# Routing records ten rows apart, tiles of successive ranks, and weighted rows written as one piece, in a fused attention and mixture-of-experts kernel

## The chip, the cores and the metric

The kernel runs on one core of a Trainium2 chip. The metric is device time in microseconds (us), the median over runs. TensorE is PE, VectorE is DVE, ScalarE is ACT, GpSimd is POOL and SyncE is SP in the profile; PEld is TensorE's weight load.

## The reference

Two parts follow each other. Attention with pooled keys and values (8 batches, 8 heads, 576 positions of 64 numbers; keys and values are means over 8 positions) gives x, 4608 tokens of 512 numbers. Then a noisy gate picks two of eight experts per token, and each expert is a two-layer network:

```python
attn = softmax(scale * q @ k_p.T)             # k_p, v_p: mean over 8 positions
x = (attn @ v_p) as (4608, 512)
noisy = x @ w_gate + log1p(exp(x @ w_noise)) * noise
top2, top2_w = two largest of noisy, softmax of the two
for e in range(8):
    for k in range(2):
        mask = top2[:, k] == e
        h = maximum(x[mask] @ w1[e], 0)       # w1: 512 x 1024
        out[mask] += top2_w[mask, k, None] * (h @ w2[e])   # w2: 1024 x 512
```

## The kernel before, in words

**Attention.** The batches are taken as four pairs. Each pair is nine chunks of 128 rows of q. The background work of a later batch (pooling of k and v, L230; block tiles `vbd`, L307 and L322) goes in between the chunks. For a chunk, PE makes scores `s`, DVE their maximum `mx` (L375), ACT the exponentials `ex` (L377), PE their transposes `ep` (L388) and the product `a` (L403), and DVE scales it to `xr` (L409, L410, L414), which is written to `x_dram`. L416 writes the chunk's gate logits into `lg`.

**Routing.** After a pair's last chunk, `route` (L480 on) turns `lg` into records. POOL adds the heads' logits (L490, L491), DVE starts with L494, and after the top-two choice `mb` (L544) PE counts ranks (`rk`, L571). DVE then works out, for each token and each of its two experts, the rank of the token among those of the expert, and the position of its record, `pos` (L594). A record is four words: the token, its weight, the row of the output if this is the token's second expert, and the slot in which the row of its first expert lies (the mate). The record's last word is written by L612. Then 18 indirect DMAs of POOL (`scatter`, L615: one chunk, one choice, 128 records of 16 bytes) write the records to `rec_dram`. They stand in a list, `scq`, and are issued one or two at a time during the next pair's chunks. Thirteen of a pair's scatters stand on POOL ahead of L490 and L491 of the next pair's route, five behind them. Each engine takes its instructions in order.

**Records in memory.** Expert e has ER = 4672 rows of `rec_dram`, and rank r lies in row e*ER + r. `load_recs` (L643 on) brings them to `raw` by sections of 4, 3, 2 and 1 tiles (4, 2, 3 and 1 for expert 0): in a section of n tiles that starts at tile ts, partition p of tile t gets rank ts*128 + p*n + (t - ts). The two first loads of expert 0 go on POOL after the second and the third pair; the rest, six DMAs, on SP after the fourth (L656). Tile 9 has 64 rows only; two memsets (L652) clear the rest.

**Experts.** From about 222 us PE multiplies. A group is 2 to 4 tiles of an expert. The rows of x are gathered by the records (`xg` by L683 for expert 0, `row` by L692 for the others). `stage1` (L964) makes `ph`, ACT `hh` and DVE `hl` of it (L971, L972), and `stage2` (L1071, or L1037 for an expert's last group) makes `py` or `xp`. Each product is three matmuls of reduced precision. `prev` (L992) gathers the mate's rows from `slot_dram` into `pv`, and `finish` (L1008) weights the tile and adds them, writes the result to `slot_dram` (L1012, on POOL) and scatters it to `out` (L1016, on POOL). The slot of rank r is 128 + e*1216 + r, so L1012 writes 128 rows that lie n rows apart. An expert's last group is computed for one of three numbers of columns, by how many records there are (`by_rows`, `tail`).

```python
ts, n = [x[:2] for x in (SECT if e else SECT0) if x[0] <= t][-1]
turn_of("pool", lambda: nc.gpsimd.dma_start(bass.AP(
    tensor=slot_dram.tensor, offset=slot_dram.offset + (P + e * CAP + ts * P + t - ts) * DM,
    ap=[[n * DM, np_], [1, DM]]), res[:np_]))
```

Of the kernel before, what the change touches and what calls it, by code (L numbers as in the profile page):

```python
# [19 lines left out]
def kernel(  # L20
# [36 lines left out]
    OVR = ER - CAP  # L57
    VW = D + 2 * E + 1
    assert (H, D, G, E, S, DM, NTOK) == (8, 64, 72, 8, 576, 512, 4608)

# [14 lines left out]

    x_dram = dp.tile([NTOK, DM], F32, name="x_dram")
    rec_dram = dp.tile([E * ER, RW], I32, name="rec_dram")
    slot_dram = dp.tile([P + E * ER, DM], F32, name="slot_dram")

    ident = cp.tile([P, P], F32, name="ident")  # L80
    make_identity(nc, ident)
# [395 lines left out]
    def route(pr, c0, c1, lg, psum):  # L477
# [69 lines left out]
        def word(w):  # L547
            return rec[:, :n, :, w].rearrange("p n i -> p i n")
# [55 lines left out]
        V.scalar_tensor_tensor(slot, ei, -float(OVR), jump, op0=OP.mult, op1=OP.add)  # L604
        V.tensor_add(key, key, ei)
        later = t(2, NCH)
        for i in range(2):
            V.tensor_tensor(later[:, i], key[:, i], key[:, 1 - i], op=OP.is_gt)
            V.scalar_tensor_tensor(word(3)[:, i], slot[:, 1 - i], float(P - E * OVR), later[:, i],
                                   op0=OP.add, op1=OP.mult)  # L610
        V.tensor_scalar(later, later, -BIG, BIG + float(pr * 2 * S), op0=OP.mult, op1=OP.add)
        V.tensor_add(word(2), later, tb)  # L612
# [17 lines left out]
            for i in range(2):  # L630
                scq.append(lambda c=c, i=i: scatter(c, i))
        if pr == NP // 2 - 1:
            scq.append(lambda: load_recs(0, 1, 0, 1, 1))
            scq.append(lambda: fetch(groups[0]))
        if pr == NP - 2:
            scq.append(lambda: load_recs(0, 1, 1, 2, 2))
            scq.append(lambda: fetch(groups[1]))
        if pr == NP - 1:
            scq.append(lambda: load_recs(0, 1, 2, 4))
            scq.append(lambda: fetch(groups[2]))  # L640
            scq.append(lambda: load_recs(1, E, 0, 4))

    def load_recs(e0, e1, s0, s1, early=0):  # L643
        ne = e1 - e0
        sect = SECT if e0 else SECT0
        t0, t1 = sect[s0][0], sect[s1 - 1][0] + sect[s1 - 1][1]
        nt = t1 - t0
        nm = f"{e0}_{t0}"
        V = nc.vector
# [3 lines left out]
        src = rec_dram.rearrange("(e r) c -> e (r c)", e=E)  # L653
        for ts, n, np_ in sect[s0:s1]:
            o = ts * P * RW
            ld = (nc.gpsimd if RE >> (0 if early else 1 if e0 == 0 else 2) & 1 else nc.sync).dma_start(raw[:np_, :, ts - t0:ts - t0 + n].rearrange("p e t c -> p e (t c)"),  # L656
                                   src[e0:e1, o:o + np_ * n * RW].rearrange("e (p x) -> p e x", p=np_))
            if early:
                tc.add_to_no_dep_group(f"rec_load{early - 1}", ld.ins)
# [337 lines left out]
    def finish(e, t, np_, y, pv, plain=0):  # L997
        res = y if plain else pv
        wc = wcol[e, t][:plain or np_]
        if not plain:  # L1000
            rv = res[:np_].rearrange("p (u m c) -> p u m c", u=4, c=32)
            yv = y[:np_].rearrange("p (m u c) -> p u m c", u=4, c=32)
            parts = [(rv[:, u], yv[:, u]) for u in range(4)]
        else:
            parts = [(res[:plain], y[:plain])]
        for r_, y_ in parts:
            if e:
                nc.vector.scalar_tensor_tensor(r_, y_, wc, pv[:plain] if plain else r_, op0=OP.mult, op1=OP.add)  # L1008
            else:
                pace[0] = nc.vector.tensor_scalar(r_, y_, wc, None, op0=OP.mult)  # L1010
        ts, n = [x[:2] for x in (SECT if e else SECT0) if x[0] <= t][-1]
        turn_of("pool", lambda: nc.gpsimd.dma_start(bass.AP(  # L1012
            tensor=slot_dram.tensor, offset=slot_dram.offset + (P + e * CAP + ts * P + t - ts) * DM,
            ap=[[n * DM, np_], [1, DM]]), res[:np_]))
# [149 lines left out]
    nc.vector.tensor_scalar(sg[:, 0:1], red[:, 0:1], float(ER), float(CAP), op0=OP.mult, op1=OP.add)  # L1164
    nc.vector.scalar_tensor_tensor(sg[:, 0:1], sg[:, 1:2], float(P), sg[:, 0:1], op0=OP.mult, op1=OP.add)
    NTAB = 64
    nc.vector.scalar_tensor_tensor(sg[:, 1:2], red[:, 0:1], -float(CAP), sg[:, 0:1], op0=OP.mult, op1=OP.add)
    nc.vector.tensor_single_scalar(sg[:, 1:2], sg[:, 1:2], float(P + (E - 1) * CAP), op=OP.add)
# [21 lines left out]
    with tc.For_i(0, totr, 1) as it:  # L1190
# [1 line left out]
                             max_val=E * ER - P)  # L1192
        er = nc.values_load(tabr[0:1, bass.ds(it * 3 + 1, 1)], engines=[SPE], min_val=0, max_val=E - 1)
        slot = nc.values_load(tabr[0:1, bass.ds(it * 3 + 2, 1)], engines=[SPE], min_val=P + E * CAP,
                              max_val=E * ER)
# [64 lines left out]
```

## Time and profile before

| What | Value |
| --- | --- |
| runs | 1083.31, 1078.56, 1077.47 us; median 1078.56 |
| profiled execution, its own time | 1077.82 us |
| its span in the trace | 1076.0 us |
| mean granted clock of PE | 0.972 |
| busy share of PE, DVE, ACT, POOL | 94%, 51%, 32%, 35% |
| chain that ended last: PE, DMA, DVE, issue, ACT, POOL | 79%, 6%, 5%, 4%, 3%, 2% |

The busy shares say that PE is close to always at work. The chain that ended last follows the work back from the end: a share of it on an engine other than PE is time in which that engine, and not PE, set the end. A row of a timeline gives start, duration, engine, line, operation, output<-input, and in brackets how long the engine had been idle and what ended that.

### The profile page before, as it was taken

The numbers are of one execution on the slowest core, as the hardware profiler recorded it, in microseconds if no ns is written. First come the engines' busy times: TensorE is split into PE (matmuls) and PEld (weight loads), VectorE is DVE, ScalarE is ACT, GpSimd is POOL, SyncE is SP. The second block draws the span as 40 slices with busy tenths as digits, with TensorE's granted clock in tenths as the row PEclk, the third lists the DMA queues.
The fourth block names the chain that finished last, engine by engine and source line by source line (L and its number), as shares of the span: only waits on it lengthen the run. The fifth ranks groups of instructions, "written<-read, shape, count | busy, mean of one in ns | idle before, by whom it ended". The sixth has DMA issues, their size and how long they took to land.

```text
span 1076.0 us, 16501 instructions
## 1 busy us (share of the span) xinstructions
PE 1006.3 (94%) x5832; PEld 895.7 (83%) x5832; DVE 548.1 (51%) x1261; ACT 347.6 (32%) x857; POOL 375.7 (35%) x421
## 2 busy tenths in 40 slices
PE   7889788889899999999999999999999999999996
PEld 6778777668789898889898988898889888988895
DVE  5678675576134463563346435634463446455342
ACT  4677657533122231332133213221322132223120
POOL 3002735445610234154214530633063305431414
PEclk8999999889899999999999999999999999999998
DMA  9999842545351776476446754764377447754623
GB/s 268 234 265 250 223 130 61 146 112 166 83 150 44 198 235 185 134 231 209 135 116 215 237 149 130 246 218 140 111 250 229 146 116 238 241 164 144 199 95 131
DMA packets 136006, 187.61 MB, mean 174 GB/s; under 512 B 29123, under 2 KB 84052, under 8 KB 135898
## 3 DMA queue, kind: packets, MB, share of 16 engines
q1 hardware_dynamic: 110458, 119.09, 39.2%
q0 software_dynamic: 25440, 67.05, 20.2%
q8 instruction: 72, 1.18, 0.5%
q14 instruction: 36, 0.29, 0.1%
HBM read 123.31 MB, written 70.74 MB: 180 GB/s over the span
## 4 chain that ended last, share of the span: by engine, by line
PE 79%; DMA 6%; DVE 5%; issue 4%; ACT 3%; POOL 2%; SPq 0%; another core or an unknown queue 0%; POOLq 0%; ACTq 0%; DVEq 0%
PE ph L964 36%; PE py L1071 16%; PE xp L1071 9%; PE py L1037 6%; PE xp L1037 3%; PE a L403 2%; DMA wst<-in_moe_w_dram 2%; DMA qr<-in_q_dram 2%; PE qp L342 1%; PE s L370 1%; PE ep L388 1%; DMA v<-in_v_dram 1%; ACT ex L377 1%; DVE w L464 1%; DVE k L230 1%
## 5 line engine op out<-in xcount | busy, mean ns | idle before, releaser
L964 PE MATMUL ph<-xh,w 128*128 128x512 f32 (+6 forms) x1536 | 400.6, 342 | 19.9 <-DVE hl L972 14.8
L964 PEld LDWEIGHTS ph<-xh,w 128*128 128x128 f32 x1536 | 275.3, 191 | 46.6 <-issue 13.7
L964 PE MATMUL ph<-xl,w 128*128 128x512 f32 (+6 forms) x768 | 262.0, 341 | 0.2
L971 ACT ACTIVATE hh<-ph 128x512 fp32r<-128x512 f32 (+4 forms) x192 | 97.6, 509 | 495.8 <-PE ph L964 346.2
L972 DVE SCALAR_TENSOR_TENSOR hl<-ph,hh 128x512 fp32r<-128x512 f32 (+4 forms) x192 | 110.0, 579 | 226.5 <-ACT hh L971 197.5
L1071 PE MATMUL py<-w,hh 128*128 128x512 f32 x592 | 184.6, 390 | 0.0
L964 PEld LDWEIGHTS ph<-xl,w 128*128 128x128 f32 x768 | 146.3, 190 | 12.3 <-issue 1.1
L1071 PEld LDWEIGHTS py<-w,hh 128*128 128x128 f32 x592 | 110.6, 188 | 21.9
L1071 PE MATMUL py<-w,hl 128*128 128x512 f32 x296 | 115.4, 390 | 0.0
L615 POOL DMA_INDIRECT rec_dram<-rec,pos x72 | 79.1, 1098 | 66.5 <-issue 14.6
L1012 POOL DMA_DIRECT2D slot_dram<-pv x55 | 31.8, 579 | 184.7 <-DVE pv L1008 157.1
L1008 DVE SCALAR_TENSOR_TENSOR pv<-py,raw,pv 128x128 f32<-128x128 f32 x124 | 35.1, 342 | 110.9 <-PE py L1071 65.8
L1012 POOL DMA_DIRECT2D slot_dram<-yt x17 | 9.8, 577 | 229.5 <-DVE yt L1008 176.2
L1071 PE MATMUL xp<-w,hh 128*128 128x512 f32 x288 | 89.5, 390 | 0.0
L992 POOL DMA_INDIRECT pv<-slot_dram,raw x70 | 68.1, 972 | 59.6 <-DMA slot_dram<-ys 33.3
L464 DVE TENSOR_TENSOR w<-wst,w 128x512 fp32r<-128x512 f32 x128 | 84.2, 695 | 7.8 <-ACT w L463 6.5
L463 ACT CAST w<-wst 128x512 fp32r<-128x512 f32 x128 | 72.7, 617 | 21.5 <-DMA wst<-in_moe_w_dram 20.9
L692 POOL DMA_INDIRECT row<-x_dram,raw x70 | 70.6, 1008 | 21.6 <-issue 21.0
L403 PE MATMUL a<-vbd,eT 112*128 112x162 f32 (+3 forms) x480 | 70.8, 313 | 5.4 <-ACT eT L390 2.8
L377 ACT ACTIVATE ex<-s,mx 128x72 f32<-128x72 f32 x288 | 70.0, 338 | 17.9 <-DVE mx L375 14.4
L403 PEld LDWEIGHTS a<-vbd,eT 112*128 112x128 f32 (+1 forms) x480 | 64.1, 195 | 9.7 <-ACT eT L390 5.1
L898 ACT CAST xh<-xt 128x512 fp32r<-128x512 f32 (+1 forms) x70 | 42.0, 600 | 91.8 <-DVE xt L893 61.0
(168 smaller groups left out, 1324.5 us busy)
## 6 DMA issues: line engine op xcount, KB each, us to landing
wst<-in_moe_w_dram SPq DMA_DIRECT2D x64, 512.0 KB
via<-row SPq DMA_DIRECT2D x266, 64.0 KB
xg<-via SPq DMA_DIRECT2D x63, 256.0 KB
slot_dram<-pv POOLq DMA_DIRECT2D x55, 256.0 KB
x_dram<-xr SPq DMA_DIRECT2D x16, 512.0 KB
q<-in_q_dram SPq DMA_DIRECT2D x7, 1024.0 KB
k<-in_k_dram SPq DMA_DIRECT2D x6, 896.0 KB
v<-in_v_dram SPq DMA_DIRECT2D x12, 432.0 KB
```

What stands on the lines that cost most here:

```text
L377: lasta[0] = nc.scalar.activation(ex[:, jj, EPOS[h] * G:(EPOS[h] + 1) * G], sv[:, i], AF.Exp, bias=mx[:, i:i + 1])
L403: nc.tensor.matmul(a[ts_, half, (hs[0] % 4) * VW:(hs[-1] % 4 + 1) * VW], eT[:BST, n, ts_], vb[:BST, SLOT0[n]:SLOT0[n] + len(hs), :], start ...
L463: nc.scalar.copy(hv, sv)
L464: nc.vector.tensor_sub(lv, sv, hv.bitcast(F32))
L615: s = nc.gpsimd.indirect_dma_start(out=rec_dram[:, :], out_offset=bass.IndirectOffsetOnAxis(ap=pos[:, i, c:c + 1], axis=0), in_=rec[:, c, ...
L692: turn_of("pool", lambda: nc.gpsimd.indirect_dma_start(out=row[:32 * nr], out_offset=None, in_=x_dram[:, :], in_offset=bass.IndirectOffset ...
L964: nc.tensor.matmul(part(ph), w1s(e, a, db, f), part(xs[b][:, db]), start=(i == 0), stop=(i == 3 * NDB - 1))
L971: act = nc.scalar.activation(hh[:, :n], ph[:, :n], AF.Relu)
L972: last = nc.vector.scalar_tensor_tensor(hl[:, :n], ph[:, :n], 0.0, hh[:, :n].bitcast(F32), op0=OP.max, op1=OP.subtract)
L992: turn_of("pool", lambda: nc.gpsimd.indirect_dma_start(out=pv[:np_], out_offset=None, in_=slot_dram[:P + e * CAP, :], in_offset=bass.Indir ...
L1037: nc.tensor.matmul(part(py), w2s(e, b, f)[:, mb * P:(mb + 1) * P], part(hs[f][a]), start=(i == 0), stop=(i == 3 * NFB - 1))
L1071: mm = nc.tensor.matmul(py, hs[f][a][:, cs], w2s(e, b, f), start=(i == 0), stop=(i == 3 * NFB - 1))
```

## The change

Rank r below 1216 now has its record in row e*ER + (r mod 128)*10 + r div 128, so successive ranks lie ten records apart, and partition p of tile t gets rank t*128 + p. Ranks from 1216 on move up by 64 rows (GAP); ER becomes 4736. `pos` needs r mod 128 and so a cast, an AND and more arithmetic: ten DVE instructions (L595 to L608) stand where three stood (L594 to L597), each of 128x18. `raw` is loaded with one DMA per call, so SP has two instead of six, and the memsets are gone. L1012 becomes a write of consecutive rows. Slot numbers are the same. The narrowest form of `tail` takes one run of columns: 368 instead of 3 pieces of 124 for expert 0, and 240 instead of 2 of 120 for the others. Where the pad is written, 592 instead of 584 KB are. The cut diff:

```diff
-    ER = CAP + OV_T * P
+    NT = 10
+    GAP = NT * P - CAP
+    ER = CAP + GAP + OV_T * P
...
+        rr = t(2, NCH)
+        V.scalar_tensor_tensor(rr, ei, -float(ER), pf, op0=OP.mult, op1=OP.add)
+        V.tensor_scalar(key, rr, float(CAP + E * ER), float(E), op0=OP.is_ge, op1=OP.mult)
+        low = t(2, NCH, dt=I32)
+        V.tensor_copy(low, rr)
+        V.tensor_single_scalar(low, low, P - 1, op=OP.bitwise_and)
+        lin = t(2, NCH)
+        V.scalar_tensor_tensor(lin, low, float(NT * P - 1), rr, op0=OP.mult, op1=OP.add)
+        V.scalar_tensor_tensor(lin, ei, float(P * ER), lin, op0=OP.mult, op1=OP.add)
+        V.tensor_scalar(lin, lin, 1.0 / P, float(E * ER - E * ER // P), op0=OP.mult, op1=OP.add)
+        far = t(2, NCH)
+        V.scalar_tensor_tensor(far, pf, float(GAP), lin, op0=OP.add, op1=OP.subtract)
+        V.scalar_tensor_tensor(far, far, 1.0 / E, key, op0=OP.mult, op1=OP.mult)
-        V.tensor_copy(pos[:, :, :n], pf)
-        key = t(2, NCH)
-        V.scalar_tensor_tensor(key, ei, -float(ER), pf, op0=OP.mult, op1=OP.add)
-        V.tensor_scalar(key, key, float(CAP + E * ER), float(E), op0=OP.is_ge, op1=OP.mult)
+        V.tensor_add(pos[:, :, :n], lin, far)
...
-        if s1 == len(SECT):
-            V.memset(raw[64:, :, nt - 1, :], 0)
-        for ts, n, np_ in sect[s0:s1]:
-            ld = (...).dma_start(raw[:np_, :, ts - t0:ts - t0 + n]..., src[e0:e1, o:o + np_ * n * RW]...)
+        src = rec_dram.rearrange("(e r) c -> e (r c)", e=E)[e0:e1, :NT * P * RW]
+        ld = (nc.gpsimd if early else nc.sync).dma_start(
+            raw.rearrange("p e t c -> p e (t c)"),
+            src.rearrange("e (p x) -> p e x", p=P)[:, :, t0 * RW:t1 * RW])
...
-        if w == 80:
-            n = 120 if e else 124
-            return ap[:, :k * P].rearrange("p (t c) -> p t c", c=P)[:, :, :n]
         return ap[:, :k * P + 64 - w]
...
+        r0 = P + e * CAP + t * P
+        turn_of("pool", lambda: nc.gpsimd.dma_start(slot_dram[r0:r0 + np_], res[:np_]))
```

A scheduler decides where the routing's DVE instructions stand among those of the attention. POOL has the same instructions in the same order as before up to the expert stage. On DVE the order moves. First the end of the first pair's route, before (`rec` is the record, L612 its last word; the names that end in numbers are of single tiles):

```order
L609 SCALAR_TENSOR_TENSOR rec_0_1003<-rt_0_24_1155,rt_0_25_1158 128x9 x2
L416 TENSOR_TENSOR lg_848<-a_2_2_0_1225,rd_2_2_0_1238 128x128
L611 TENSOR_SCALAR rt_0_25_1158<-rt_0_25_1158 128x18
L375 TENSOR_REDUCE mx_3_1_0_1266<-s_3_1_0_1262 128x6
L612 TENSOR_TENSOR rec_0_1003<-rt_0_25_1158,tok_107 128x2x9
L375 TENSOR_REDUCE mx_3_1_1_1279<-s_3_1_1_1275 128x6
L307 TENSOR_TENSOR vbd_163<-vs_1121,vmask 112x8x64
L409 TENSOR_SCALAR rd_3_0_0_1295<-a_3_0_0_1288 128x8
L307 TENSOR_TENSOR vbd_163<-vs_1121,vmask 112x2x64
L410 RECIPROCAL rd_3_0_0_1295<-rd_3_0_0_1295 128x8
L230 TENSOR_TENSOR k_189<-k_189 128x5x128
```

The same place on DVE in the changed kernel, where `pos` is L608 and the record's last word L623:

```order
L375 TENSOR_REDUCE mx_3_1_1_1290<-s_3_1_1_1286 128x6
L608 TENSOR_TENSOR pos_0_1160<-rt_0_25_1153,rt_0_26_1157 128x18
L616 TENSOR_TENSOR rt_0_22_1146<-rt_0_22_1146,rt_0_9_981 128x18
L307 TENSOR_TENSOR vbd_163<-vs_1121,vmask 112x8x64
L619 TENSOR_TENSOR rt_0_29_1169<-rt_0_22_1146 128x9 x2
L409 TENSOR_SCALAR rd_3_0_0_1306<-a_3_0_0_1299 128x8
L620 SCALAR_TENSOR_TENSOR rec_0_1003<-rt_0_28_1166,rt_0_29_1169 128x9 x2
L410 RECIPROCAL rd_3_0_0_1306<-rd_3_0_0_1306 128x8
L622 TENSOR_SCALAR rt_0_29_1169<-rt_0_29_1169 128x18
L307 TENSOR_TENSOR vbd_163<-vs_1121,vmask 112x2x64
L623 TENSOR_TENSOR rec_0_1003<-rt_0_29_1169,tok_107 128x2x9
L414 TENSOR_TENSOR xr_3_0_0_1309<-a_3_0_0_1299,rd_3_0_0_1306 128x512
```

The record's last word has moved behind `mx_3_1_1`, both parts of `vbd_163`, `rd_3_0_0` and its reciprocal. The second pair's route on DVE, before:

```order
L307 TENSOR_TENSOR vbd_163<-vs_1770,vmask 112x8x64
L609 SCALAR_TENSOR_TENSOR rec_0_1651<-rt_0_24_1802,rt_0_25_1805 128x9 x2
L375 TENSOR_REDUCE mx_5_0_2_1853<-s_5_0_2_1850 128x4
L611 TENSOR_SCALAR rt_0_25_1805<-rt_0_25_1805 128x18
L409 TENSOR_SCALAR rd_4_2_0_1885<-a_4_2_0_1872 128x8
L612 TENSOR_TENSOR rec_0_1651<-rt_0_25_1805,tok_107 128x2x9
L307 TENSOR_TENSOR vbd_163<-vs_1770,vmask 112x2x64
L410 RECIPROCAL rd_4_2_0_1885<-rd_4_2_0_1885 128x8
L230 TENSOR_TENSOR v_194<-v_194 112x6x256
```

and in the changed kernel:

```order
L307 TENSOR_TENSOR vbd_163<-vs_1781,vmask 112x2x64
L608 TENSOR_TENSOR pos_0_1818<-rt_0_25_1811,rt_0_26_1815 128x18
L616 TENSOR_TENSOR rt_0_22_1804<-rt_0_22_1804,rt_0_9_1640 128x18
L375 TENSOR_REDUCE mx_5_1_1_1946<-s_5_1_1_1942 128x6
L619 TENSOR_TENSOR rt_0_29_1827<-rt_0_22_1804 128x9 x2
L230 TENSOR_TENSOR v_194<-v_194 112x6x256
L620 SCALAR_TENSOR_TENSOR rec_0_1662<-rt_0_28_1824,rt_0_29_1827 128x9 x2
L409 TENSOR_SCALAR rd_5_0_0_1962<-a_5_0_0_1955 128x8
L622 TENSOR_SCALAR rt_0_29_1827<-rt_0_29_1827 128x18
L375 TENSOR_REDUCE mx_5_1_2_1994<-s_5_1_2_1991 128x4
L623 TENSOR_TENSOR rec_0_1662<-rt_0_29_1827,tok_107 128x2x9
L410 RECIPROCAL rd_5_0_0_1962<-rd_5_0_0_1962 128x8
```

Here the record's last word has moved behind the pooling of v (L230) and behind two later maxima, `mx_5_1_1` and `mx_5_1_2`.

## Rows read from the trace of the kernel before

**Rows 1.** The page's busy table: busy us (share of the span), instructions.

```profile
PE 1006.3 (94%) x5832; PEld 895.7 (83%) x5832; DVE 548.1 (51%) x1261; ACT 347.6 (32%) x857; POOL 375.7 (35%) x421
```

**Rows 2.** Busy time by stretch: length, engines, granted PE clock, DMA share, GB/s.

```profile
303.00:1036.00 733.00, 716.81 (x3898) 641.85 (x3897) 347.16 (x654) 182.71 (x342) 243.92 (x266) 1.00 0.58 176
```

**Rows 3.** Timeline of POOL, the first pair's scatters.

```profile
99.60 1.16 POOL L615 DMA_INDIRECT rec_dram<-rec,pos  x1 [8.54 <-DVE rec L612]
...
102.92 2.51 POOL L615 DMA_INDIRECT rec_dram<-rec,pos  x1 [0.30 <-issue]
...
120.38 2.28 POOL L490 TENSOR_TENSOR lg<-lg 128x576 f32<-128x576 f32 x2
122.74 0.49 POOL L491 TENSOR_TENSOR rt<-lg 128x144 f32<-128x144 f32 x1
```

**Rows 4.** Timeline of DVE, the end of the first pair's route.

```profile
99.11 0.18 DVE L612 TENSOR_TENSOR rec<-rt,tok 128x18 int32<-128x18 f32 x1
99.20 0.60 DVE L375 TENSOR_REDUCE mx<-s 128x6 f32<-128x432 f32 x1
99.72 0.68 DVE L307 TENSOR_TENSOR vbd<-vs,vmask 112x512 f32<-112x512 f32 x1
100.59 0.17 DVE L409 TENSOR_SCALAR rd<-a 128x8 f32<-128x8 f32 x1 [0.20 <-issue]
...
100.98 0.77 DVE L230 TENSOR_TENSOR k<-k 128x640 f32<-128x640 f32 x1
...
123.26 0.23 DVE L494 SCALAR_TENSOR_TENSOR rt<-rt 128x72 f32<-128x72 f32 x1 [3.35 <-POOL rt L491]
```

**Rows 5.** Timeline of PE behind the two routes' starts.

```profile
125.98 0.65 PE L388 MATMUL ep<-ident,ex 128*112 128x128 f32 x4 [0.88 <-ACT qT L344]
...
175.80 0.65 PE L388 MATMUL ep<-ident,ex 128*112 128x128 f32 x4 [0.26 <-issue]
```

**Rows 6.** Timeline of POOL, the second pair's scatters.

```profile
147.40 2.49 POOL L615 DMA_INDIRECT rec_dram<-rec,pos  x1 [6.92 <-DVE vbd L307]
...
162.64 1.11 POOL L615 DMA_INDIRECT rec_dram<-rec,pos  x1 [2.76 <-ACT ex L377]
...
169.04 0.97 POOL L615 DMA_INDIRECT rec_dram<-rec,pos  x1 [0.89 <-DVE lg L416]
170.03 2.30 POOL L490 TENSOR_TENSOR lg<-lg 128x576 f32<-128x576 f32 x2
```

**Rows 7.** Timeline of DVE, behind the end of the second pair's route.

```profile
147.33 1.71 DVE L230 TENSOR_TENSOR v<-v 112x1536 f32<-112x1536 f32 x1
...
154.45 0.46 DVE L375 TENSOR_REDUCE mx<-s 128x4 f32<-128x288 f32 x1 [1.61 <-PE s L370]
```

**Rows 8.** Timeline of POOL, the last of the third pair's scatters ahead of L490.

```profile
217.47 0.97 POOL L615 DMA_INDIRECT rec_dram<-rec,pos  x1 [2.39 <-DVE lg L416]
```

**Rows 9.** Busy time by stretch around a fall of the granted clock.

```profile
136.00:140.00 4.00, 1.94 (x20) 1.76 (x19) 4.00 (x20) 0.21 (x1) 0.00 (x0) 1.00 0.69 262
140.00:144.00 4.00, 3.67 (x32) 2.78 (x32) 3.72 (x21) 3.45 (x12) 0.11 (x1) 0.75 0.10 37
144.00:148.00 4.00, 4.00 (x35) 3.21 (x32) 2.45 (x10) 2.09 (x10) 0.60 (x1) 0.82 0.87 262
```

**Rows 10.** DMA queues in 1053.45:1054.12 (first) and 1069.9:1071.1: packets, MB, share.

```profile
q0 software_dynamic: 50, 0.19, 74.2%
...
q0 software_dynamic: 79, 0.26, 58.3%
```

**Rows 11.** Waits of all engines in 303:1036: total us, times, longest.

```profile
PE ph L964 <- DVE hl L972: 12.6, 7, 2.5
```

**Rows 12.** Groups of instructions by shape, expert 0's last group.

```profile
L964 PE MATMUL ph<-xh,w 128*128 128x372 f32 x64 | 17.7, 355 | 2.5 <-DVE hl L972 2.5
```

**Rows 13.** Timelines of SP and of PE, the late record loads and what needs them.

```profile
283.62 3.47 SPq L656 DMA_DIRECT2D raw<-rec_dram  x6
...
295.30 1.12 PE L887 MATMUL xp<-ident,xg 128*128 128x128 f32 x8
```

More of the change, by code (lines that the diff above doesn't have):

```diff
@@ L56 @@
     RW = 4
-    OVR = ER - CAP
+    OVR = OV_T * P
     VW = D + 2 * E + 1
@@ L77 @@
     rec_dram = dp.tile([E * ER, RW], I32, name="rec_dram")
-    slot_dram = dp.tile([P + E * ER, DM], F32, name="slot_dram")
+    slot_dram = dp.tile([P + E * (CAP + OVR), DM], F32, name="slot_dram")
     ident = cp.tile([P, P], F32, name="ident")
@@ L592, in route @@
             V.tensor_reduce(out=pf[:, i], in_=pm, axis=AX, op=OP.add)
+        key = t(2, NCH)
+        rr = t(2, NCH)
[11 more added lines that the diff above has]
+        V.scalar_tensor_tensor(far, far, 1.0 / E, key, op0=OP.mult, op1=OP.mult)
         pos = rp.tile([P, 2, NCH], I32, tag="pos", name=f"pos{pr}_{c0}", bufs=4)
-        V.tensor_copy(pos[:, :, :n], pf)
-        key = t(2, NCH)
-        V.scalar_tensor_tensor(key, ei, -float(ER), pf, op0=OP.mult, op1=OP.add)
-        V.tensor_scalar(key, key, float(CAP + E * ER), float(E), op0=OP.is_ge, op1=OP.mult)
+        V.tensor_add(pos[:, :, :n], lin, far)
         jump = t(2, NCH)
@@ L603, in route @@
         slot = t(2, NCH)
-        V.scalar_tensor_tensor(slot, ei, -float(OVR), jump, op0=OP.mult, op1=OP.add)
+        V.scalar_tensor_tensor(slot, ei, -float(ER - CAP), jump, op0=OP.mult, op1=OP.add)
         V.tensor_add(key, key, ei)
@@ L608, in route @@
             V.tensor_tensor(later[:, i], key[:, i], key[:, 1 - i], op=OP.is_gt)
-            V.scalar_tensor_tensor(word(3)[:, i], slot[:, 1 - i], float(P - E * OVR), later[:, i],
+            V.scalar_tensor_tensor(word(3)[:, i], slot[:, 1 - i], float(P - E * (ER - CAP)), later[:, i],
                                    op0=OP.add, op1=OP.mult)
@@ L632, in route, with load_recs @@
         if pr == NP // 2 - 1:
-            scq.append(lambda: load_recs(0, 1, 0, 1, 1))
+            scq.append(lambda: load_recs(0, 1, 0, 4, 1))
             scq.append(lambda: fetch(groups[0]))
         if pr == NP - 2:
-            scq.append(lambda: load_recs(0, 1, 1, 2, 2))
+            scq.append(lambda: load_recs(0, 1, 4, 6, 2))
             scq.append(lambda: fetch(groups[1]))
         if pr == NP - 1:
-            scq.append(lambda: load_recs(0, 1, 2, 4))
+            scq.append(lambda: load_recs(0, 1, 6, NT))
             scq.append(lambda: fetch(groups[2]))
-            scq.append(lambda: load_recs(1, E, 0, 4))
-    def load_recs(e0, e1, s0, s1, early=0):
+            scq.append(lambda: load_recs(1, E, 0, NT))
+    def load_recs(e0, e1, t0, t1, early=0):
         ne = e1 - e0
-        sect = SECT if e0 else SECT0
-        t0, t1 = sect[s0][0], sect[s1 - 1][0] + sect[s1 - 1][1]
         nt = t1 - t0
         nm = f"{e0}_{t0}"
-        V = nc.vector
         raw = rp.tile([P, ne, nt, RW], I32, name=f"raw{nm}")
-        if s1 == len(SECT):
-            V.memset(raw[64:, :, nt - 1, :], 0)
-        src = rec_dram.rearrange("(e r) c -> e (r c)", e=E)
-        for ts, n, np_ in sect[s0:s1]:
[L655 to L659, printed above, removed]
+        src = rec_dram.rearrange("(e r) c -> e (r c)", e=E)[e0:e1, :NT * P * RW]
+        ld = (nc.gpsimd if early else nc.sync).dma_start(
+            raw.rearrange("p e t c -> p e (t c)"),
+            src.rearrange("e (p x) -> p e x", p=P)[:, :, t0 * RW:t1 * RW])
+        if early:
+            tc.add_to_no_dep_group(f"rec_load{early - 1}", ld.ins)
         for e in range(e0, e1):
@@ L1010, in finish @@
                 pace[0] = nc.vector.tensor_scalar(r_, y_, wc, None, op0=OP.mult)
[L1011 to L1014, printed above, removed]
+        r0 = P + e * CAP + t * P
+        turn_of("pool", lambda: nc.gpsimd.dma_start(slot_dram[r0:r0 + np_], res[:np_]))
         if e:
@@ L1163 @@
     nc.vector.tensor_sub(sg[:, 1:2], prow, red[:, 1:2])
-    nc.vector.tensor_scalar(sg[:, 0:1], red[:, 0:1], float(ER), float(CAP), op0=OP.mult, op1=OP.add)
+    nc.vector.tensor_scalar(sg[:, 0:1], red[:, 0:1], float(ER), float(CAP + GAP), op0=OP.mult, op1=OP.add)
     nc.vector.scalar_tensor_tensor(sg[:, 0:1], sg[:, 1:2], float(P), sg[:, 0:1], op0=OP.mult, op1=OP.add)
     NTAB = 64
-    nc.vector.scalar_tensor_tensor(sg[:, 1:2], red[:, 0:1], -float(CAP), sg[:, 0:1], op0=OP.mult, op1=OP.add)
-    nc.vector.tensor_single_scalar(sg[:, 1:2], sg[:, 1:2], float(P + (E - 1) * CAP), op=OP.add)
+    nc.vector.scalar_tensor_tensor(sg[:, 1:2], red[:, 0:1], -float(CAP + GAP), sg[:, 0:1], op0=OP.mult, op1=OP.add)
+    nc.vector.tensor_single_scalar(sg[:, 1:2], sg[:, 1:2], float(P + (E - 1) * CAP - GAP), op=OP.add)
     tab = rp.tile([P, 3], I32, name="tab")
@@ L1194 @@
         slot = nc.values_load(tabr[0:1, bass.ds(it * 3 + 2, 1)], engines=[SPE], min_val=P + E * CAP,
-                              max_val=E * ER)
+                              max_val=E * (CAP + OVR))
         rec = op.tile([P, RW], I32, name="orec")
```

2 lines of the change are left out of this document (removed).

## The prediction

> **What bounds the kernel now.** I read the page's busy table first, then busy time by stretch, then the timelines of POOL, DVE and PE where the routing is. PE is busy for 94% of the span [rows 1], and in the expert stage from 303 to 1036 us for 716.81 of 733.00 us [rows 2]. There the end is set by PE's matmuls, whose number this change leaves alone. Before that, to about 222 us, the attention is paced by a ring of PE, DVE, ACT and POOL, and a delay on one of them reaches PE. The place to see it is POOL's timeline of the first pair's scatters: they begin at 99.60, released by the record's last word on DVE after 8.54 us of idle time; thirteen follow one another, and only then POOL does L490 and L491 of the next route, at 120.38 and 122.74 [rows 3]. DVE, which works in order, stands at L494 for 3.35 us until L491 is done, at 123.26 [rows 4], and behind L494 lie the maximum, the exponentials and the transposes of the next chunk, for which PE idles 0.88 us [rows 5]. So whatever makes the first pair's record late makes L494 late, and PE with it.
>
> **The sum, part by part.** It is made against the profiled execution's own 1077.82 us, which is 0.74 below the median of 1078.56.
>
> *First pair's record.* In the new order five attention instructions stand ahead of the record's last word that stood behind it. In the old trace they fill the stretch from 99.20 to 100.98 [rows 4], 1.78 us. Seven more small instructions are to be done too. One of 128x18 lasts 0.18 us, but the next one starts 0.09 us after it [rows 4], so seven cost 0.63 us at that pace, or 1.26 if each had its whole duration to itself. Some of them may fall into holes in which DVE waits anyway, so the bounds are 1.8 and 3.0 us. I take 2.1, nearer the lower end since the new instructions are interleaved with longer ones. POOL has no slack in this stretch: scatters stand 0.30 us apart and its L491 ends DVE's wait. The whole 2.1 us therefore reach L494 and PE. What is late next is everything of the attention behind it, which shifts as one.
>
> *Second pair's record.* Here the last word moves further: behind a pooling of v of 1.71 us and behind a maximum that starts at 154.45 because it waits 1.61 us for PE [rows 7]. The first scatter went at 147.40 [rows 6]. It can't go before the maximum is done, 154.45 + 0.46 and some 0.3 for the last words and the release: 155.2, which is 7.8 us later. Before, the thirteen scatters weren't back to back: they were held back for 2.76 and 0.89 us, among others, by the pace that the list sets, and the first took 2.49 [rows 6]. At the shortest cadence of the rows, 0.97 + 0.30 us, thirteen take 16.5 us, and L490 starts at 171.7 in place of 170.03 [rows 6], 1.7 later. PE's next wait was only 0.26 us, with nothing that held it but its own issue [rows 5]. I take 1.4 for it, with bounds of 0 (the tail of the list keeps its pace and catches up) and 6.0 (the second rival).
>
> *Third and fourth pair.* The last of the third pair's scatters ahead of L490 waits 2.39 us for the pace, not for the record [rows 8], so about 2.4 us of lateness would be hidden there, and the record moves by about that. The fourth route runs beside PE's matmuls. Seven small instructions are 0.63 us of DVE, and only where PE waits for `hl` could they count, 12.6 us in seven places of the whole stage [rows 11]. I take 0 for both, with 0.6 as the bound.
>
> *Record loads.* SP issues two DMAs instead of six; the six take 3.47 us from 283.62 on, and PE's transposes of what is gathered by them begin at 295.30 without any wait [rows 13]. An earlier landing is therefore worth nothing, and a landing later by a few us too; without that cover the 3.47 us would be the price. The memsets stood at DVE's start and on no path; the pad's 8 KB more, of 592, are too little to be seen.
>
> *The write as one piece.* The same 128 rows of 2 KB go out with one instruction of POOL as before. The write of an expert's last 64 rows was contiguous already, and the profile has it apart: in the window around it 50 packets took 74.2% of 16 engines in 0.67 us, so 0.159 us each; around a write with rows three apart 79 packets took 58.3% in 1.2 us, 0.142 us each [rows 10]. Each packet is about 4 KB in the first and somewhat less in the second, which has part of a scatter in it. The contiguous one isn't cheaper, so I give it 0; in the expert stage PE, not the queue, sets the pace. [...]
>
> *Columns.* Expert 0's last group goes from 372 to 368 columns in 192 matmuls (64 and 32 in the first stage and 96 in the second). One of 372 lasts 355 ns [rows 12], 0.95 ns per column at most, since matmuls overlap; four columns in 192 are 0.7 us at most. I take 0.3.
>
> Sum: 2.1 + 1.4 - 0.3 = +3.2, so 1077.82 + 3.2 = **1081.0 us**. That is 0.23% above the median shown. About 0.5%, or 5.4 us, is what a measurement of this kernel can tell from no change: faster is below 1073.2 here, slower above 1083.9.
>
> **The rivals.**
>
> *Hidden.* The attention may have more slack than the chain shows: the pace of later scatters, and the wider DVE instructions that the new order moves behind the record, could give the 3.5 us back by the end of the stage. Then only the columns are left, 1077.82 - 0.3 = 1077.5. For it: the order lets DVE do other work in what were 3.35 us of idle time at L494. Against it: PE itself waited behind L494 in the old trace [rows 5].
>
> *Slower: the second pair's scatters run at the first pair's cadence.* The mechanism sits on POOL between 155 and 176 us. Scatters take up to 2.51 us where DVE does wide additions at the same time [rows 3], and the first pair's thirteen took 20.78 us, from 99.60 to 120.38. If the late second block, now packed into the stretch with the next additions, goes at that cadence, L490 starts at 155.2 + 20.8 = 176.0, which is 6.0 us late, 5.7 after PE's 0.26. The time is 1077.82 + 2.1 + 5.7 - 0.3 = 1085.3. It decides as soon as the mean cadence is above about 1.5 us. Against it: the last of the old block took 0.97 us [rows 6]. [...]
>
> [...]
>
> *Faster: transfers land sooner.* PE waits for `hl` in seven places of the expert stage, 12.6 us in all [rows 11], where DVE is behind the weighting of an earlier tile. If whole pieces and loads with fewer pieces, or gathers of neighbouring tokens, halve that, 6.3 us are saved: 1081.0 - 6.3 = 1074.7. Against it: the rows show no gain for a contiguous write [rows 10], and the longest single wait is 2.5 us.
>
> **How the numbers follow.** I give the forecast 0.45, hidden 0.22, the clock 0.10, the slow scatters 0.11 and sooner transfers 0.12. The range reaches from 1076.0, below the hidden case, to 1085.5, which takes in the slow scatters; it leaves out most of the case of sooner transfers and the outer parts of the others, less than 0.2 together. The forecast, the hidden case and the clock lie within 0.5%, and sooner transfers lie half outside. That gives 0.05 for faster, 0.83 for the same, 0.12 for slower.
>
> **What would show it.** On POOL the first scatter at about 101.7 instead of 99.60 and L490 at about 122.5; DVE's wait at L494 longer than 3.35 us, near 5; PE's wait of 0.88 us near 3. In the second pair the first scatter near 157 on the shifted clock, 13 of them at about 1.3 us, and L490 near 173.8. The first expert matmul about 3.5 us later, and the stretch behind it as long as before within 0.5 us. The forecast is wrong if L490 of either route starts where it did, if the attention ends no later than before, or if the expert stage changes by more than 2 us: then the transfers, not the routing, made the difference.

## The result, and the profile after

The changed kernel's median is 1083.06 us (1080.87 to 1085.06, 7 runs); before stood at 1077.47 beside it (1074.97 to 1083.78, 7 runs). The ratio is 1.0057, with an interval of 1.0034 to 1.0080: slower by 0.57%. The forecast of 1081.0 lies 2 us below, and the range holds the time. The ratio is just past the 0.5% that were to count as no change, and its interval has that line inside; the time itself stays below the 1083.9 us from which the prediction counted "slower", a case that had 0.12.

The profiled execution took 1083.51 us, with a span of 1081.7. Of the changed kernel's page, the lines of busy time, the first DMA queue and the chain that ended last:

```profile
PE 1011.5 (94%) x5832; PEld 901.7 (83%) x5832; DVE 549.2 (51%) x1287; ACT 348.1 (32%) x857; POOL 368.2 (34%) x421
...
q1 hardware_dynamic: 108090, 119.11, 37.3%
...
PE 79%; DVE 7%; issue 4%; ACT 4%; DMA 3%; POOL 1%; another core or an unknown queue 1%; SPq 1%; POOLq 0%; ACTq 0%; DVEq 0%
```

The busy shares are those of before [rows 1], within 1%. In the chain DMA has gone from 6% to 3% and DVE from 5% to 7%, and 1%, where the page of before has 0%, is ended by something that the profile can't name. It is the entry to remember. The loads with fewer pieces show in the queue, 108090 packets for 110458.

Where the time went is read from busy time by stretch (PE, PEld, DVE, ACT, POOL, then PE's granted clock, DMA share, GB/s). After:

```profile
60.00:222.00 162.00, 136.38 (x1058) 124.07 (x1058) 110.86 (x366) 103.42 (x352) 58.81 (x62) 0.89 0.59 172
100.00:140.00 40.00, 33.23 (x249) 31.10 (x247) 26.75 (x75) 23.64 (x79) 20.57 (x21) 0.87 0.77 223
140.00:180.00 40.00, 32.27 (x229) 29.58 (x229) 23.45 (x80) 23.96 (x84) 16.93 (x18) 0.83 0.22 74
303.00:1036.00 733.00, 715.55 (x3882) 638.93 (x3881) 347.14 (x654) 183.74 (x345) 241.94 (x266) 1.00 0.57 177
```

and the attention's stretches before, with the same columns:

```profile
60.00:222.00 162.00, 134.13 (x1068) 119.31 (x1067) 113.43 (x352) 103.93 (x351) 69.44 (x67) 0.92 0.65 178
100.00:140.00 40.00, 31.80 (x275) 29.12 (x273) 30.40 (x85) 26.00 (x89) 25.75 (x21) 1.00 0.85 239
140.00:180.00 40.00, 35.48 (x295) 31.00 (x293) 24.01 (x78) 28.25 (x99) 22.23 (x22) 0.96 0.29 86
```

The expert stage is as full as it was [rows 2]. The attention got fewer matmuls done in the same time (249 and 229 for 275 and 295), at a lower clock. From the first pair's rank count to the first expert matmul (the first `ph`) it took 140.5 us instead of 133.3, and from there to the last matmul 845.1 instead of 843.7. Both numbers differ by some us from one execution of the same kernel to the next: another trace of before, taken later, has 125.5 and 846.8.

### The profile page after: what moved, and what is told of

Read it like the earlier page. It is cut to its first block, busy times and chain, and to the rows that moved or that the text cites. A ratio compares the mean times of both kernels' runs of the same rounds, so it can differ in the third digit from the quotient of the medians.

```text
span 1081.7 us, 16517 instructions
## 1 busy us (share of the span) xinstructions
PE 1011.5 (94%) x5832; PEld 901.7 (83%) x5832; DVE 549.2 (51%) x1287; ACT 348.1 (32%) x857; POOL 368.2 (34%) x421
## 3 DMA queue, kind: packets, MB, share of 16 engines
q1 hardware_dynamic: 108090, 119.11, 37.3%
## 4 chain that ended last, share of the span: by engine, by line
PE 79%; DVE 7%; issue 4%; ACT 4%; DMA 3%; POOL 1%; another core or an unknown queue 1%; SPq 1%; POOLq 0%; ACTq 0%; DVEq 0%
PE ph L966 36%; PE py L1071 16%; PE xp L1071 9%; PE py L1037 6%; PE a L403 4%; PE xp L1037 3%; PE ep L388 2%; ACT ex L377 1%; PE qp L342 1%; PE s L370 1%; DMA wst<-in_moe_w_dram 1%; DMA v<-in_v_dram 1%; ACT eT L390 1%; DVE w L464 1%
## 5 line engine op out<-in xcount | busy, mean ns | idle before, releaser
L626 POOL DMA_INDIRECT rec_dram<-rec,pos x72 | 73.7, 1024 | 81.8 <-DVE rec L623 16.8
L377 ACT ACTIVATE ex<-s,mx 128x72 f32<-128x72 f32 x288 | 70.0, 338 | 18.3 <-DVE mx L375 16.2
L403 PEld LDWEIGHTS a<-vbd,eT 112*128 112x128 f32 (+1 forms) x480 | 66.7, 199 | 9.0 <-ACT eT L390 7.0
```

Of the source, the lines that this page charges most:

```text
L377: lasta[0] = nc.scalar.activation(ex[:, jj, EPOS[h] * G:(EPOS[h] + 1) * G], sv[:, i], AF.Exp, bias=mx[:, i:i + 1])
L403: nc.tensor.matmul(a[ts_, half, (hs[0] % 4) * VW:(hs[-1] % 4 + 1) * VW], eT[:BST, n, ts_], vb[:BST, SLOT0[n]:SLOT0[n] + len(hs), :], start ...
L626: s = nc.gpsimd.indirect_dma_start(out=rec_dram[:, :], out_offset=bass.IndirectOffsetOnAxis(ap=pos[:, i, c:c + 1], axis=0), in_=rec[:, c, ...
```

## POOL was late as forecast, DVE did not wait, PE did

POOL's timeline of the changed kernel, the first and last rows of both blocks of thirteen scatters, and L490 behind each:

```profile
98.94 1.16 POOL L626 DMA_INDIRECT rec_dram<-rec,pos  x1 [10.67 <-DVE rec L623]
...
121.31 2.29 POOL L490 TENSOR_TENSOR lg<-lg 128x576 f32<-128x576 f32 x2
...
152.86 1.49 POOL L626 DMA_INDIRECT rec_dram<-rec,pos  x1 [11.96 <-DVE rd L410]
...
171.65 0.99 POOL L626 DMA_INDIRECT rec_dram<-rec,pos  x1 [4.53 <-ACT ex L377]
...
175.38 2.28 POOL L490 TENSOR_TENSOR lg<-lg 128x576 f32<-128x576 f32 x2
```

This execution's first rank count is 2.8 us earlier than that of before. So the first scatter is 101.7 on the old clock, where 99.60 stood [rows 3] and 101.7 was forecast. In the second pair POOL waited 11.96 us for the record, where 6.92 stood [rows 6]: counted from its pair's rank count, that scatter is 5.0 us later than before. But DVE's L494, where the delay was to come through, on DVE's timeline:

```profile
124.92 0.22 DVE L494 SCALAR_TENSOR_TENSOR rt<-rt 128x72 f32<-128x72 f32 x1
...
178.26 0.23 DVE L494 SCALAR_TENSOR_TENSOR rt<-rt 128x72 f32<-128x72 f32 x1 [0.48 <-POOL rt L491]
```

The first has no wait where 3.35 us stood [rows 4]: DVE itself was late by then. What made it late is in the timeline of all engines around 110 us:

```profile
106.96 0.66 PE L370 MATMUL s<-kbd,qT 128*128 128x144 f32 x4
107.18 0.97 POOL L626 DMA_INDIRECT rec_dram<-rec,pos  x1 [0.30 <-issue]
108.46 0.97 POOL L626 DMA_INDIRECT rec_dram<-rec,pos  x1 [0.30 <-issue]
109.73 0.97 POOL L626 DMA_INDIRECT rec_dram<-rec,pos  x1 [0.30 <-issue]
110.52 0.17 DVE L409 TENSOR_SCALAR rd<-a 128x8 f32<-128x8 f32 x1 [3.71 <-remote]
...
112.09 0.59 ACT L390 COPY eT<-ep 112x512 f32<-112x512 f32 x1 [4.28 <-remote]
...
112.73 0.68 PE L388 MATMUL ep<-ident,ex 128*112 128x128 f32 x2 [5.11 <-ACT eT L390]
```

PE, DVE and ACT all stand from 107.8 to 110.5 us, and of the engines that compute POOL alone goes on, issuing scatters 0.30 us apart. (`eT` is ACT's copy of the transposes `ep`.) DVE waits for the product `a`, whose matmuls end by 106.40 in the records, ACT for `ep`, whose matmuls end by 107.12; they get on at 110.52 and 112.09. The releaser "remote" is a signal that the profile can't tie to an instruction. In the trace's semaphore events PE's own semaphore has no update between 106.11 and 110.50. This trace has lost some of these events (it keeps 591 of the 645 that PE's instructions make), so the hole alone proves little; but DVE goes on 0.02 us after the update at 110.50. The chain of waits calls the same stretch by the name seen above, and the second pair has its like 52 us later. The chain of the changed kernel, from 100 to 120 and from 154 to 172:

```profile
106.85 0.96 ACT ex L377 x4
107.81 4.21 another core or an unknown queue
...
157.57 2.02 ACT ex L377 x9
159.59 4.97 another core or an unknown queue
```

```profile
165.28 0.68 PE L388 MATMUL ep<-ident,ex 128*112 128x128 f32 x2 [5.29 <-ACT eT L390]
```

That last row is PE's timeline after the second stretch. PE waits 5.11 and 5.29 us at the same instruction of two pairs, and each time the granted clock falls from 1.00 to 0.50 before the wait is over, and stays there: from 112.1 to 122.3 and from 163.3 to 176.9 us. At the same place of the first pair the old trace has this row:

```profile
111.07 0.43 PE L388 MATMUL ep<-ident,ex 128*112 128x128 f32 x2 [1.27 <-issue]
```

Three theories were set against each other: the arithmetic, that is the longer routing on DVE and the order that comes of it; the memory, that is the new places of write, loads and gathers; and the chance of a single execution. By the names of their instructions, the traces of before and of the change differ in order not on DVE alone but on PE and ACT too, on both from about 110 us on; where "the order" is named below, all three are meant. In every comparison below, before ran on the same chip beside the kernel; the ratios are those on record and differ by up to 0.3% from the quotients of the medians. Each round has a chip of its own. The change itself ran on the first round's chip for one trace, and on the other two not at all: that its two waits would come there too is not shown.

## First round: which part of the change costs it

**The change again, one trace.** No edit.

> The changed kernel once more, for its trace alone. Routing theory (the seven more small instructions and the new places of the routing on DVE cost the time): PE again idles about 5 us at the transposes near 113 and near 165 us, and the first expert matmul comes near 228. Chance theory (those two waits belong to that one execution): they are absent or elsewhere, and the first expert matmul comes 3 us or more away from 228.

Measured: 1086.18 us. PE's timeline of this trace:

```profile
116.49 0.68 PE L388 MATMUL ep<-ident,ex 128*112 128x128 f32 x2 [5.00 <-ACT eT L390]
...
168.64 0.68 PE L388 MATMUL ep<-ident,ex 128*112 128x128 f32 x2 [6.01 <-issue]
```

The same two waits at the same two places: chance falls. The attention's stretch of this trace has a granted clock of 0.93, where the first trace of the change has 0.89 and that of before 0.92:

```profile
60.00:222.00 162.00, 133.10 (x1066) 120.27 (x1065) 112.84 (x368) 104.02 (x354) 60.79 (x62) 0.93 0.60 175
```

**The arithmetic alone.** The kernel before, with the ten instructions of the new `pos`, whose constants are set so that the old row comes out. Loads, write and layout are the old ones.

```diff
-        V.tensor_copy(pos[:, :, :n], pf)
...
+        rr = t(2, NCH)
+        V.scalar_tensor_tensor(rr, ei, -float(ER), pf, op0=OP.mult, op1=OP.add)
...
+        V.tensor_copy(low, rr)
+        V.tensor_single_scalar(low, low, P - 1, op=OP.bitwise_and)
...
+        V.scalar_tensor_tensor(lin, low, 0.0, rr, op0=OP.mult, op1=OP.add)
...
+        V.tensor_add(pos[:, :, :n], lin, far)
```

> The kernel before with the changed kernel's ten DVE instructions for the record's row, whose constants here give the old row; record loads, slot writes and columns as before. Routing theory: as slow as the changed kernel, ratio 1.004 to 1.007, with PE's two waits near 113 and 165 us. Memory theory (the one-piece write, the loads with 160-byte runs and the gathers of neighbouring tokens cost the time): ratio 1.000, within 0.002.

Measured: 1086.72 us (1083.85 to 1089.88, 6 runs) against 1076.75 (18 runs), ratio 1.0090 (1.0059 to 1.0121). On PE's timeline:

```profile
119.47 0.68 PE L388 MATMUL ep<-ident,ex 128*112 128x128 f32 x2 [5.33 <-ACT eT L390]
...
173.04 0.67 PE L388 MATMUL ep<-ident,ex 128*112 128x128 f32 x2 [6.00 <-ACT eT L390]
```

The whole loss, and both waits, come without any new place in memory: the arithmetic holds, and memory falls as the cause. By the medians it costs 10 us, more than the whole change. That something else in the change gains does not follow from this pair: 1.0059 to 1.0121 and the change's 1.0034 to 1.0080 overlap. The third round comes back to it.

**The old write.** The changed kernel with the writes that lie n rows apart.

```diff
-        r0 = P + e * CAP + t * P
-        turn_of("pool", lambda: nc.gpsimd.dma_start(slot_dram[r0:r0 + np_], res[:np_]))
+        ts, n = [...][-1]
+        turn_of("pool", lambda: nc.gpsimd.dma_start(bass.AP(..., ap=[[n * DM, np_], [1, DM]]), res[:np_]))
```

> The changed kernel with the old write of the slots, whose rows lie up to four rows apart; so the rows that a later expert reads as mates are not the right ones, their number and size are the same. Routing theory: as the changed kernel, ratio to the kernel before 1.004 to 1.007. Memory theory: most of the loss goes, ratio below 1.002.

Measured: 1085.50 us (1080.73 to 1091.57, 7 runs), ratio 1.0086 (1.0052 to 1.0119), PE's waits of 5.07 us at 117.14 and 5.28 at 169.64. Against the change's own 1.0057 the write would be worth 0.3%, but the intervals overlap; that it alone gains is not shown.

**The route ahead of the attention's work.** The changed kernel; the scheduler is told to put the arithmetic from `rank` to the record's last word sooner.

```diff
+        with tc.high_priority(offset=40):
-        rank = t(NCH, E)
+            rank = t(NCH, E)
...
-        V.tensor_add(word(2), later, tb)
+            V.tensor_add(word(2), later, tb)
```

> The changed kernel with the routing's last block, from the ranks to the record's last word, put 40 places ahead in the scheduler's order: the second pair's record then stands ahead of the pooling of v and of two maxima, the first pair's ahead of the smaller vbd part. Routing theory: the second pair's first scatter comes 5 us earlier, the PE wait near 165 us shrinks to below 2 us, and the ratio falls to 1.000 to 1.003. Memory theory: ratio 1.004 to 1.007 as the changed kernel.

Measured: 1081.08 us (1074.07 to 1088.73, 12 runs), ratio 1.0032 (1.0002 to 1.0061). PE's timeline:

```profile
119.57 0.78 PE L320 MATMUL vr<-wrb,vT 128*112 128x64 f32 x6 [3.20 <-issue]
...
165.04 0.43 PE L388 MATMUL ep<-ident,ex 128*112 128x128 f32 x2 [1.13 <-ACT vT L315]
```

The second wait shrinks to 1.13 us, and from the second to the third pair's rank count the trace takes 45.0 us instead of 52.1. The first keeps 3.20, at another instruction. This goes with the records: counted from the rank count, the first scatter is 4.3 us sooner than in the change in the second pair (8.2 for 12.6), and no sooner in the first (11.2 for 11.3). The order is a part of the cause. By the medians moving it by hand cures about half, but the interval overlaps with the change's, so how much is not shown.

## Second round: are the scatters needed for it

**Before again, one trace.** No edit.

> The kernel before once more, for its trace alone. Order theory (the long waits belong to the order of the instructions): as in its first trace no PE wait above 2.2 us between 100 and 170 us, while all traces of the new order have two of 5 to 6. Chance theory: a wait of 4 us or more there.

Measured: 1070.53 us; before's median on this chip was 1069.73 (21 runs). PE's longest wait between 100 and 180 us is between what the two theories expected:

```profile
114.53 1.10 PE L388 MATMUL ep<-ident,ex 128*112 128x128 f32 x4 [2.69 <-ACT qT L344]
```

The old order has none of 5 us on this chip either.

**The new kernel without the scatters of two pairs.**

```diff
-                scq.append(lambda c=c, i=i: scatter(c, i))
+                scq.append((lambda c=c, i=i: scatter(c, i)) if pr > 1 else (lambda: None))
```

> The changed kernel without the scatters of the first two pairs' records (their places in the list are kept; half of the records keep the pad's content, so the tokens that are gathered for them are others, in the same number). Collision theory (the loss is in the scatters, and PE's two waits of 5 us come with them): both waits fall below 1.5 us, the time falls by 8 us or more against the changed kernel, and is within 0.2% of the next kernel's. Order theory without scatters (the seven instructions and the later places on DVE cost the time by themselves): it stays 0.4% or more above the next kernel.

**The old kernel with the same edit.**

> The kernel before without the scatters of the first two pairs' records, in the same manner. Collision theory: ratio 0.993 to 0.998 to the kernel before, for the waits of 0.9 to 2.1 us that it has there. Order theory: ratio 0.998 to 1.001.

Measured: the new 1054.47 us (1053.35 to 1058.57, 6 runs), ratio 0.9881 (0.9844 to 0.9918); the old 1062.68 (1057.35 to 1066.90, 12 runs), 0.9939 (0.9912 to 0.9967). Busy time in the attention's stretch, first of the new kernel and then of the old, both without those scatters:

```profile
60.00:222.00 162.00, 144.65 (x1174) 129.10 (x1173) 128.74 (x420) 114.07 (x379) 32.46 (x37) 0.97 0.64 187
```

```profile
60.00:222.00 162.00, 137.82 (x1104) 122.39 (x1103) 119.39 (x381) 107.03 (x360) 30.34 (x36) 0.95 0.66 182
```

Without scatters there is no wait of over 2 us on PE between 100 and 200, and the new kernel, with all its extra arithmetic, does more in the stretch (1174 matmuls for 1104) and is the faster one, by 0.6% (0.9881/0.9939) where the collision theory had the two within 0.2%. So the seven instructions can cost little by themselves: from the first rank count to the first expert matmul the new kernel takes 114.0 us and the old 118.7, though the layout differs too. By these traces what costs is the new order together with scatters in flight: in that stretch, leaving them out saves 24 to 26 us in the new kernel (137.8 and 140.5 to 114.0) and 7 to 15 in the old (125.5 and 133.3 to 118.7). The two traces of the change are from other chips.

**Shorter arithmetic for the same rows.** The changed kernel; one conversion of (r - 63.5)/128, which came out as r div 128 in this run, stands in place of cast, AND and what follows. Six instructions where ten stood, `pos` among the first.

```diff
-        low = t(2, NCH, dt=I32)
-        V.tensor_copy(low, rr)
-        V.tensor_single_scalar(low, low, P - 1, op=OP.bitwise_and)
+        hi = t(2, NCH, dt=I32)
+        V.tensor_scalar(hi, rr, 1.0 / P, -(E * ER + 63.5) / P, op0=OP.mult, op1=OP.add)
...
+        V.tensor_scalar(lin, pf, float(NT), -float((NT - 1) * E * ER), op0=OP.mult, op1=OP.add)
+        V.scalar_tensor_tensor(lin, ei, -float((NT - 1) * ER), lin, op0=OP.mult, op1=OP.add)
...
-        V.tensor_add(pos[:, :, :n], lin, far)
+        V.scalar_tensor_tensor(pos[:, :, :n], hi, -float(NT * P - 1), lin, op0=OP.mult, op1=OP.add)
```

> The changed kernel with a shorter way to the record's row: the quotient by one rounded conversion, six DVE instructions where it has ten and the kernel before three; the case of more than 1216 records for an expert, which these inputs don't have, is left out. Loads, writes and columns as changed. In the scheduler's order the record's last word then stands ahead of the maxima and poolings again. Routing theory: ratio 0.998 to 1.001, no PE wait above 2.5 us between 100 and 170 us. Memory theory: 1.004 to 1.008 as the changed kernel.

Measured: 1058.55 us (1056.08 to 1061.71, 10 runs), ratio 0.9910 (0.9883 to 0.9938): by its ratio faster than both kernels, and than either theory expected. POOL's timeline, where the record's last word is L618, and the attention's busy time:

```profile
96.31 1.31 POOL L621 DMA_INDIRECT rec_dram<-rec,pos  x1 [8.63 <-DVE rec L618]
...
115.48 2.29 POOL L490 TENSOR_TENSOR lg<-lg 128x576 f32<-128x576 f32 x2
...
139.39 0.97 POOL L621 DMA_INDIRECT rec_dram<-rec,pos  x1 [6.53 <-DVE rec L618]
...
157.65 2.29 POOL L490 TENSOR_TENSOR lg<-lg 128x576 f32<-128x576 f32 x2
```

```profile
60.00:222.00 162.00, 142.04 (x1133) 126.12 (x1132) 122.95 (x395) 108.79 (x365) 71.98 (x73) 0.95 0.59 176
```

The scatters are as dense here, mostly 0.30 us apart, in blocks of 19.2 and 18.3 us. Yet PE's longest wait between 100 and 180 us is the first of these rows:

```profile
126.34 0.43 PE L388 MATMUL ep<-ident,ex 128*112 128x128 f32 x2 [1.17 <-ACT eT L390]
...
183.98 1.10 PE L388 MATMUL ep<-ident,ex 128*112 128x128 f32 x3 [3.70 <-ACT ex L377]
```

The second row, just behind, is a wait of another kind: 3.70 us for ACT's `ex`, not for `eT`. So density alone does not make the long waits; it matters where the attention's instructions stand beside the scatters.

## Third round: the layout by itself, and a later start

**The old rows with the short arithmetic.** The kernel before with six instructions as above, their constants giving the old row.

```diff
-        V.tensor_copy(pos[:, :, :n], pf)
...
+        V.tensor_scalar(hi, rr, 1.0 / P, -(E * ER + 63.5) / P, op0=OP.mult, op1=OP.add)
...
+        V.tensor_scalar(lin, pf, 1.0, 0.0, op0=OP.mult, op1=OP.add)
+        V.scalar_tensor_tensor(lin, ei, 0.0, lin, op0=OP.mult, op1=OP.add)
...
+        V.scalar_tensor_tensor(pos[:, :, :n], hi, 0.0, lin, op0=OP.mult, op1=OP.add)
```

> The kernel before (old rows, loads and writes) with the six instructions of the short arithmetic, whose constants here give the old row; its DVE order is close to that of the fast kernel e8. Order theory (e8 beats the kernel before because its records stand earlier among the attention's instructions): ratio 0.988 to 0.995. Layout theory (new rows, loads and writes give e8's gain): ratio 0.998 to 1.002.

Measured: 1072.31 us (1067.97 to 1075.05, 12 runs) against 1076.27 (29 runs), ratio 0.9963 (0.9943 to 0.9982). Three more instructions than before, and faster: again the order, not their duration. Against 0.9910 for the same arithmetic with the new rows, the layout (rows, loads, write and columns together) is worth 0.9910/0.9963 = 0.9947, some 5.7 us; the two intervals don't overlap. The two ratios come from two chips. The order is not what parts these kernels: by the names of their instructions ACT and POOL have the same order in both traces, PE the same but for one matmul of the expert stage, and DVE the same in the attention from 90 us on.

**The old kernel with its route ahead.** The edit of the priority, made to the kernel before.

> The kernel before with the routing's last block, from the ranks to the record's last word, 40 places ahead in the scheduler's order and nothing else changed. Order theory: ratio 0.988 to 0.996, the attention ends 5 us or more earlier. Layout theory: ratio 0.998 to 1.002.

Measured: 1077.22 us (12 runs), ratio 1.0006 (0.9987 to 1.0026). Counted from the rank counts, the first scatters come 0.8 and 1.6 us sooner than before, and nothing is gained: sooner records don't help as such, in a kernel without the long waits.

**Scatters four entries later.** The changed kernel; empty entries ahead of the scatters of the first two pairs, so nine instead of thirteen stand ahead of L490.

```diff
+        if pr < 2:
+            scq.extend([lambda: None] * 4)
```

> The changed kernel with its DVE order near the place as it is, but the scatters of the first two pairs start four places later in their list, so nine instead of thirteen stand ahead of the next route's L490. If scatters in flight at one place of the order make PE's waits of 5 us, the one near 113 us shrinks to below 2 us and the ratio is 0.992 to 1.001. If the waits come from the DVE order alone, they stay above 4 us and the ratio is 1.004 to 1.009.

Measured: 1084.60 us (1077.39 to 1088.68, 12 runs), ratio 1.0067 (1.0046 to 1.0088). The waits of 5 us are gone, and from the first rank count to the first expert matmul the trace takes 127.4 us. The longest wait between 100 and 180 us:

```profile
159.60 0.43 PE L388 MATMUL ep<-ident,ex 128*112 128x128 f32 x2 [1.34 <-ACT eT L390]
```

PE, DVE and ACT have the instructions of the change here in the very same order; only POOL's differs. So the order of these three alone does not make the waits. But the time comes back behind it. PE's waits from 230 us on, in this kernel (total, times, longest):

```profile
PE ph L968 <- DVE hl L976: 15.5, 7, 5.4
PE ph L968 <- issue: 7.7, 6, 3.2
PE xp L894 <- DMA xg<-x_dram,raw: 5.5, 1, 5.5
```

PE now stands 5.5 us for rows gathered by the records, where the changed kernel has 0.6, and 5.4 once for `hl`, where its longest is 2.2. PE is busy for 67.80 of the 81 us from 222 to 303, for 73.97 in the change. Starting the scatters later shortens the attention and starves the first expert, and the ratio that the collision theory expected is missed; it does not tell what holds PE.

**Short arithmetic and the route ahead.** Both edits on the changed kernel.

> The short arithmetic of e8 and the routing's last block put ahead in the order as in e4. Order theory: as e8 or up to 0.2% faster, ratio 0.988 to 0.993. If e8 was a lucky order, it falls back above 0.996.

Measured: 1067.42 us (1064.83 to 1073.31, 6 runs), ratio 0.9920 (0.9894 to 0.9947), no better than the short arithmetic alone.

| Kernel | Rows | Arithmetic of `pos` and `key` | Ratio to before |
| --- | --- | --- | --- |
| the change | new | ten | 1.0057 |
| arithmetic alone | old | ten | 1.0090 |
| route ahead | new | ten | 1.0032 |
| short | new | six | 0.9910 |
| short | old | six | 0.9963 |
| two pairs without scatters | new | ten | 0.9881 |
| two pairs without scatters | old | three | 0.9939 |

## Why the prediction was right in the sum and wrong in its terms

*The records' delay* was right for the first scatter, 2.1 us later. The second block began behind the maximum and the pooling as forecast, but 5.0 us later instead of 7.8, since that maximum did not wait for PE this time. L490 then came 3.7 and 4.9 us later, counted from the rank counts, where 2.1 and 1.7 were summed: the scatters waited for the attention in between. The thirteen of the second block took 22.5 us from the first scatter to L490, above the 20.8 of the rival of slow scatters, but not for its reason. Ten of the first eleven lasted 0.97 us each, the one at 154.66 too, beside which DVE's addition L236 ran from 155.16 to 155.99, so DVE's additions did not slow these; 4.53 and 1.75 us of waiting for the attention came near the end.

*"The whole 2.1 us therefore reach L494 and PE"* is the step that failed. L494's wait went to 0 and 0.48. The delay came in upstream of it, as two waits of PE of 5.11 and 5.29 us for `eT`. The arithmetic and its order cost 10 us by the run of the arithmetic alone, by the medians, where 3.5 were summed. I followed POOL's lateness to the one DVE instruction that had waited for POOL, and never asked what the shifted scatters would lie beside.

*The clock* was given 0.10, for one fall more like that of rows 9, which lost 4 x 0.25 + 4 x 0.18 = 1.7 us of full clock there, so 1082.7. It took part. At half clock for 10.2 and 13.6 us, PE has a granted clock of 0.89 between 60 and 222 us instead of 0.92: 162 x 0.03 = 5 us of full clock, an estimate from single traces. The second trace of the change has 0.93 there with the same two waits, so how much the clock took is open. Both long waits, of 5.11 and 5.29 us, ended at a granted clock of 0.50; the old trace's wait of 1.27 us at the same place of the first pair left it at 1.00. The runs do not part the waits from the half clock that comes with them.

*Write, loads and columns* at -0.3 us were undersized. Like against like, the new places are worth 1.0057/1.0090 = 0.9967 with ten instructions, which is not clear of noise, and 0.9947 with six, which is, so 3.5 to 5.7 us. The route put ahead in the short arithmetic with the new rows gives 0.9920/0.9963 = 0.9957 against the short one with the old rows, on one chip but in another order, and the pair without scatters 0.9881/0.9939 = 0.9942, with another arithmetic. The size is near that of the rival of sooner transfers, 6.3 below the forecast, which had 0.12; its mechanism is not shown. PE's waits for `hl` from 230 us on are 10.1 us both in before's second trace and in that of the short arithmetic, which are from one chip. Whether write, loads or gathers make the gain stays open: no run parts them well enough. The expert stage of the single traces does not show it for the change itself (843.7 and 846.8 us before, 845.1 and 846.5 after).

So, by the medians, 10 us lost and some 4 won gave +5.6 where +3.2 was forecast. The sum was near because two terms that were both too small have opposite signs. That is luck.

## What to carry to other kernels

Count small instructions by where they push others, not by their own duration: here seven of 0.18 us cost nothing that could be seen without the scatters and, by the medians, 10 us with them, and with six in another form the same change was 0.9% faster than before. Before accepting such a change, write the arithmetic in its shortest form, with the word that the next engine waits for first, and look at the order that the scheduler then makes. To judge a layout, run the new index arithmetic on the old layout: only that comparison showed that the layout gained while the change lost.

## What the runs showed of the hardware

Not expected: stretches, in the first trace of the change, in which PE stands for 5.1 and 5.3 us, ACT for 4.3 and 5.1 and DVE for 3.7 and 3.6 (all three at once for 2.7 and 1.7) while POOL issues scatters, with DVE going on at 110.52 for matmuls that the records end by 106.40, and a releaser that the trace can't name. The long waits of PE, of 5.0 to 6.0 us, came in four traces of three kernels at the same place of the program (the change twice, the arithmetic alone, the old write). They were gone without scatters (1.9 us at most from 100 to 200 us), with the order of the short arithmetic (1.17 us at most from 100 to 180) and with later scatters (1.34 there), in traces from other chips; with the route put ahead one of the two was gone (1.13 us left, the other 3.20), on the chip of the first round. In the second stretch, from 160 to 165.3 us, the DMA engines moved nothing but 160 packets of scatters, 2 GB/s and 3.2% of 16 engines, no load of instructions either, so the bandwidth is not what is short there. The ends of matmuls in the records are modelled, so the trace doesn't say whether PE worked late or its signals came late. What holds them is open.
